# Two layers of spectral mixing and a gated-shift MLP on one core: first norm and transform by group, tables made ahead, sums on two engines, weights over all partitions

## The chip, the cores and the metric

The kernel runs on one core of a Trainium2 chip. TensorE multiplies matrices, VectorE and ScalarE work elementwise and read TensorE's results out of PSUM, GpSimd does small work here, and SyncE (SP) and ScalarE issue the transfers from memory. Each engine works through its own queue in order and waits for others by semaphores. The metric is the device time of one execution in microseconds (us), as a median of several runs.

## The reference, cut to what matters

The state `x` has 2048 rows of 512 numbers in bf16. Two equal layers follow each other. Each layer first mixes by a two-dimensional Fourier transform with a pointwise weight, then runs an MLP block with shifts along the rows:

```
x = x + A(layernorm(x))      # rfft2 over (2048, 512), times (w_r + i w_i), irfft2
x = x + B(layernorm(x))      # h = gelu(layernorm(x) @ w1); quarters of h shifted by -1, +1, -2, +2 rows, @ w2
                             # x1 = x + that; x1 + gelu(layernorm(x1) @ w3) @ w4
x = x + A(layernorm(x))
x = x + B(layernorm(x))
```

## The kernel before

Row p*16 + q of `x` lies in partition p, block q (16 blocks `x[:, q, :]` of 128x512). The transforms are matrix products with tables made on the host: `T` over the partitions, `FA` over the 512 columns, `TL` over the 16 blocks, and their inverses `TR`, `G`, `Tinv`. The norm's mean falls out of the transform, since the zero frequency of the columns is left out; its factor 1/sigma is put into `T`.

`load_all` (line 135) issues all loads: `x` in eight chunks of two blocks on SP's queue (L148), `T` and `FA` on ScalarE's (L149, L150), then on SP's `TL`, the weights `W` in 24 pieces (L157, L159, L161; one destination is 16 neighbouring partitions), `TR`, `G`, `Tinv` and the MLP's matrices. An issue waits until the transfer eight issues earlier has landed.

`first_front` (L253) works in groups of four blocks. For a group it takes the norm's sums, of two blocks in three by `bn_stats` and `bn_aggr` on VectorE (L191, L192), of the third (q % 3 == 2) by two passes of ScalarE over the block (L266) and four small operations of GpSimd (L269 to L272). Then `rstd` (L207): VectorE adds epsilon (`ln_ve`), GpSimd takes the power -1/2 (`ln_r`). One group later, `front` (L234) does for each block a scaled table `Tq` on VectorE (L238), four matmuls into `ps_V` (L241), and a copy into `V`, by turns on VectorE (L244) and ScalarE (L132).

`middle` (L282) has 16 steps b: `over_d` (matmuls from all of `V`, L294), `over_q` (L302 to L304), then in pairs of steps `weigh` (products `Pab` of X with `W` on VectorE, L317, and their sums `Z`), and `back_q` (L326, L327) `LAG = 5` steps later, copied into `M` by turns on ScalarE and VectorE. `X` has two buffers of two steps.

`mlp` (L348) is written out in steps s: `back_d(s)` (`ps_Y`, L366, copied to `Y` by ScalarE), `back_p(s-1)` (`ps_y`, L373; the addition to `x`, L374; `bn`), and after each fourth block `rstd_twice` (L214: VectorE's small operations, two powers on GpSimd giving `ln_r` and `ln_c`). `norm2(g)` scales a group into `xn` (L230) at s = 5, 9, 13, 17, `tr` transposes it (`pt`, copied to `xT` by ScalarE) two steps later, then follow `w1`, `w2`, `norm3`, `apply3`, `tr3`, `w3` and `w4`. With the last four `w4` blocks of the first layer, `fr` calls `front` for the second layer, groups in the order of `GROUPS` (L345): group 0 after the first `w4`, group 1 after the second, groups 2 and 3 after the fourth. Names in the trace are the tiles' names without numbers.

## Time and profile before

| | before |
|---|---|
| median of 3 runs | 437.0 us (434.43 to 437.14) |
| the profiled execution | 437.16 us |
| its span, first to last instruction | 435.4 us |
| TensorE busy (matmul) | 379.7 us, 87% |
| VectorE busy | 215.1 us, 49% |
| ScalarE busy | 214.3 us, 49% |
| GpSimd busy | 39.3 us, 9% |
| mean granted TensorE clock | 0.976 |

The profile is of one execution. Its span leaves out 1.76 us around the instructions. [...] A row's bracket names how long the engine was idle before it and what released it.

### The profile page before, as it was taken

To read this page: it belongs to the slowest core of one execution; us is meant where nothing else is said; L and a number is where in the kernel's file an instruction comes from. 1 tells how busy PE (TensorE), PEld (TensorE's weight loads), DVE (VectorE), ACT (ScalarE), POOL (GpSimd) and SP (SyncE) were. 2 spreads that over 40 slices of the span, in tenths; PEclk is the share of its full clock that TensorE was granted. 3 is DMA by queue.
4 is the path that set the end of the run, shared out by engine and by line. 5 is a ranking of instruction groups with operands and counts; after the bars stand their busy time and mean duration, and the time that the engine had idled before them with its cause. 6 is when DMAs were issued, how large, how long until landed. Compare 5 with 4: busy or idle time off the path is not lost.

```text
span 435.4 us, 5373 instructions
## 1 busy us (share of the span) xinstructions
PE 379.7 (87%) x2048; PEld 189.9 (44%) x2048; DVE 215.1 (49%) x547; ACT 214.3 (49%) x396; POOL 39.3 (9%) x65
## 2 busy tenths in 40 slices
PE   0237997799799999999966998979889999999996
PEld 0123663345345444444433465335444454444442
DVE  4452777987546432231535278698754641011021
ACT  3334774577766814234032576457777680514300
...
DMA packets 12219, 15.63 MB, mean 36 GB/s; under 512 B 1184, under 2 KB 10144, under 8 KB 11936
## 3 DMA queue, kind: packets, MB, share of 16 engines
...
HBM read 13.17 MB, written 2.10 MB: 35 GB/s over the span
## 4 chain that ended last, share of the span: by engine, by line
PE 75%; DVE 9%; DMA 8%; ACT 6%; issue 1%; POOL 0%; ACTq 0%; SPq 0%; DVEq 0%; POOLq 0%
PE ps_g L452 22%; PE ps_o L460 22%; PE ps_TV L294 7%; PE ps_Y L366 5%; PE ps_x L420 4%; PE ps_h L406 4%; DMA W<-in_A_w_r_dram 4%; ACT xT L132 3%; PE pt L393 2%; DVE ln_st L191 2%; DMA TR<-tab_TR 2%; PE ps_X L304 1%; DMA W<-in_A_w_i_dram 1%; DVE x_state L374 1%; PE ps_V L241 1%; ACT junk L425 1%
## 5 line engine op out<-in xcount | busy, mean ns | idle before, releaser
L452 PE MATMUL ps_g<-xT,w 128*128 128x512 bf16 x448 | 100.9, 379 | 3.1 <-ACT xT L132 3.1
L454 ACT ACTIVATE gT<-ps_g 128x512 bf16<-128x512 f32 x112 | 64.7, 604 | 67.9 <-PE ps_g L452 67.9
L460 PE MATMUL ps_o<-w,gT 128*128 128x512 bf16 x448 | 98.0, 379 | 0.0
L462 DVE TENSOR_TENSOR x_state<-ps_o,x_state 128x512 bf16<-128x512 f32 x32 | 22.1, 692 | 125.6 <-PE ps_o L460 125.6
L452 PEld LDWEIGHTS <-w 128*128 128x128 bf16 x448 | 43.6, 98 | 54.9 <-issue 3.7
L460 PEld LDWEIGHTS <-gT 128*128 128x128 bf16 x448 | 43.7, 98 | 52.5
L241 PE MATMUL ps_V<-Tq,x_state 128*128 128x128 bf16 x128 | 13.9, 276 | 34.6 <-DVE Tq L238 34.6
L191 DVE BATCH_NORM_STATS2 ln_st<-x_state 128x6 f32<-128x512 bf16 x59 | 40.8, 691 | 6.1 <-DMA x_state<-in_A_x_dram 4.4
L294 PE MATMUL ps_TV<-FA,V 128*128 128x512 bf16 x128 | 36.8, 418 | 1.6 <-DVE V L244 0.9
L366 PE MATMUL ps_Y<-G,M 128*128 128x512 bf16 x128 | 35.6, 407 | 1.9 <-DVE M L331 0.9
L406 PE MATMUL ps_h<-xT,w 128*128 128x512 bf16 x128 | 33.9, 389 | 2.7 <-ACT xT L132 2.7
L132 ACT ACTIVATE V<-ps_V 128x512 bf16<-128x512 f32 x22 | 12.1, 601 | 48.5 <-PE ps_V L241 48.5
L132 ACT ACTIVATE xT<-pt 128x1024 bf16<-128x1024 bf16 x32 | 31.1, 1032 | 5.3 <-PE pt L393 5.3
L422 DVE SCALAR_TENSOR_TENSOR xn<-xn,ln_c,ps_x 128x512 bf16<-128x512 bf16 x32 | 23.5, 745 | 20.6 <-PE ps_x L420 20.5
L317 DVE TENSOR_TENSOR Pab<-X,W 128x1024 bf16<-128x1024 bf16 x32 | 20.8, 689 | 24.4 <-ACT X L132 24.2
L420 PE MATMUL ps_x<-w,hT 128*128 128x512 bf16 x128 | 32.8, 379 | 0.0
L212 POOL TENSOR_TENSOR ln_r<-ln_ve,mhalf 128x4 f32<-128x4 f32 (+1 forms) x19 | 17.5, 923 | 154.9 <-DVE ln_ve L211 154.9
L425 ACT ACTIVATE junk<-xn 128x512 bf16<-128x512 bf16 x32 | 20.1, 629 | 21.8 <-DVE xn L422 21.7
L132 ACT ACTIVATE TV<-ps_TV 128x512 bf16<-128x512 f32 x32 | 19.1, 597 | 17.9 <-PE ps_TV L294 16.9
L241 PEld LDWEIGHTS <-x_state 128*128 128x128 bf16 x128 | 11.0, 125 | 38.1 <-issue 26.4
L132 ACT ACTIVATE Y<-ps_Y 128x512 bf16<-128x512 f32 x32 | 19.1, 598 | 16.4 <-PE ps_Y L366 16.4
L374 DVE TENSOR_TENSOR x_state<-ps_y,x_state 128x512 bf16<-128x512 f32 x32 | 21.5, 672 | 7.3 <-PE ps_y L373 7.3
...
## 6 DMA issues: line engine op xcount, KB each, us to landing
...
```

What stands on the lines that cost most here:

```text
L132: K.nc.scalar.activation(dst, src, ACT.Copy, bias=0.0, scale=1.0)
L191: v.bn_stats(st[:], src)
L241: nc.tensor.matmul(ps[:, t * P:(t + 1) * P], lhsT=K.x[:, q, t * P:(t + 1) * P], rhs=Tq[:], start=True, stop=True)
L294: nc.tensor.matmul(ps[:], lhsT=V[:, t, b].rearrange("d q c -> d (q c)"), rhs=K.FA[:, t, :], start=(t == 0), stop=(t == 3))
L366: nc.tensor.matmul(ps[:], lhsT=M[:, F, e, q, :], rhs=K.G[:, F, e, :], start=(n == 0), stop=(n == 3))
L374: nc.vector.tensor_tensor(K.x[:, q, :], ps[:], K.x[:, q, :], op=ALU.add)
L406: nc.tensor.matmul(ps[:], lhsT=K.w1[:, t, j * P:(j + 1) * P], rhs=xT[g][:, t, :], start=(t == 0), stop=(t == 3))
L420: nc.tensor.matmul(ps[:], lhsT=K.hT[:, j, st:st + P], rhs=K.w2[:, j, :], start=(j == 0), stop=(j == 3))
L425: nc.scalar.activation(junk[:], xn[:, q, :], ACT.Square, bias=0.0, scale=1.0, accum_out=ln3[g].s[:, i, 1:2])
L452: nc.tensor.matmul(ps[:], lhsT=K.w3[:, c, t * P:(t + 1) * P], rhs=xT3[g][:, c, :], start=(c == 0), stop=(c == 3))
L454: nc.scalar.activation(gT[g][:, t, :], ps[:], ACT.Gelu_apprx_tanh, bias=0.0, scale=1.0)
L460: nc.tensor.matmul(ps[:], lhsT=gT[g][:, t, i * P:(i + 1) * P], rhs=K.w4[:, t, :], start=(t == 0), stop=(t == 13))
```

## The change

Loads: `FA` moves from ScalarE's queue to SP's, behind `x`. The pieces of `W` go to partitions jj*2 + sg, in steps of 8 over all 128, instead of 16 neighbours, and the host's tables `TL` and `TR` follow that order.

First front: all of ScalarE's sums are issued first, for all groups; `scaled_T` (the table), `over_p` (the matmuls) and `take_V` (the copy) take the place of `front`, and the groups interleave, with the four tables of a group made before its matmuls. Copies: two groups by S, S, V, S, two by S, V, S, V.

Norms: `from_sums` and `rstd_twice` run on GpSimd altogether; in `back_p` every odd block's sum comes with the addition (`accum_out`) and its sum of squares from ScalarE. `norm2` comes one step later, and so do the four `apply3`.

`middle`: `LAG` is 6, the last two steps are weighed one by one, and the copies to `M` of the last steps are dealt out anew, the last of them in two halves. Passage to the second layer: tables of groups 0 and 1 before the last four `w4` blocks, of group 2 after the first, and of group 3 one by one; the last copy in two halves.

```diff
-                col = slice(jj * 32 + sg * 16, jj * 32 + sg * 16 + 16)
+                col = slice(jj * 2 + sg, P, 8)
...
     table("T", nc.scalar)
-    table("FA", nc.scalar)
+    table("FA", nc.sync)
     table("TL", nc.sync)
...
-            row = jj * 32
-            nc.sync.dma_start(K.W[row:row + 16, pl, :, :], v[jj])
-            row += 16
-            nc.sync.dma_start(K.W[row:row + 16, pl, 1:16, :], v[7 - jj][:, 1:16, :][:, ::-1, :])
+            rows = slice(jj * 2, P, 8)
+            nc.sync.dma_start(K.W[rows, pl, :, :], v[jj])
+            rows = slice(jj * 2 + 1, P, 8)
+            nc.sync.dma_start(K.W[rows, pl, 1:16, :], v[7 - jj][:, 1:16, :][:, ::-1, :])
...
+    def square(self, i, src):
+        K = self.K
+        junk = K.stream.tile([P, D], BF16, name="junk", bufs=2)
+        K.nc.scalar.activation(junk[:], src, ACT.Square, bias=0.0, scale=1.0, accum_out=self.s[:, i, 1:2])
+
+    def from_sums(self, sl):
+        e = self.K.nc.gpsimd
         t = self.K.small.tile([P, 4, 1], FP32, name="ln_t")
...
+        e.tensor_scalar(self.mv[:, sl], self.s[:, sl], 1.0 / D, None, op0=ALU.mult)
+        e.tensor_tensor(t[:, sl], self.mv[:, sl, 0:1], self.mv[:, sl, 0:1], op=ALU.mult)
+        e.tensor_tensor(self.mv[:, sl, 1:2], self.mv[:, sl, 1:2], t[:, sl], op=ALU.subtract)
...
+        e.tensor_scalar(ve2[:], self.mv[:, :, 1], 0.0, 1.0 + EPS, op0=ALU.max, op1=ALU.mult)
+        e.tensor_scalar(ve2[:], ve2[:], EPS * EPS, None, op0=ALU.add)
+        e.tensor_tensor(self.r[:], ve2[:], K.mhalf[:], op=ALU.pow)
+        e.tensor_scalar(ve[:], self.mv[:, :, 1], 0.0, EPS, op0=ALU.max, op1=ALU.add)
+        e.tensor_tensor(ve[:], ve[:], K.mhalf[:], op=ALU.pow)
+        e.tensor_tensor(ve2[:], ve2[:], self.r[:], op=ALU.mult)
+        e.tensor_tensor(self.c[:], ve2[:], ve[:], op=ALU.mult)
...
+def scaled_T(K, q, r):
+
+    K.Tq[q] = K.stream.tile([P, P], BF16, name="Tq", bufs=NQ)
+    K.nc.vector.tensor_scalar(K.Tq[q][:], K.T[:], r, None, op0=ALU.mult)
...
+def take_V(K, q, eng):
+    src = K.psV.pop(q)[:].rearrange("d (t b c) -> d t b c", t=4, c=8)
+    n = NB // len(eng)
+    for h, e in enumerate(eng):
...
+    for q in on_act:
+        g, i = divmod(q, 4)
+        if not hasattr(L[g], "s"):
+            L[g].sums()
+        junk = K.stream.tile([P, D], BF16, name="junk", bufs=2)
+        nc.scalar.activation(junk[:], K.x[:, q, :], ACT.Copy, bias=0.0, scale=1.0, accum_out=L[g].s[:, i, 0:1])
+        L[g].square(i, K.x[:, q, :])
...
+    def tables(g):
+        for i in range(4):
+            scaled_T(K, 4 * g + i, L[g].r[:, i:i + 1])
+        for i in range(4):
+            over_p(K, 4 * g + i)
+
+    def take(g):
+        for i in range(4):
+            take_V(K, 4 * g + i, "SSVS"[i] if g < 2 else "SVSV"[i])
+
+    stats(0)
+    stats(1)
+    tables(0)
+    stats(2)
+    take(0)
+    tables(1)
+    stats(3)
+    take(1)
+    tables(2)
+    take(2)
+    tables(3)
+    take(3)
...
-        if b % 2 == 1:
-            weigh(b - 1, 2, X)
+        if b >= NB - 2:
+            weigh(b, 1, X[:, b % 2:b % 2 + 1])
+        elif b % 2 == 1:
+            weigh(b - 1, 2, X[:])
...
-    LAG = 5
+    take_M = ["S", "V"] * 5 + ["V", "V", "S", "S", "S", "SV"]
+    LAG = 6
...
+        if i % 2:
+            nc.vector.scalar_tensor_tensor(K.x[:, q, :], ps[:], 1.0, K.x[:, q, :], op0=ALU.mult, op1=ALU.add,
+                                           accum_out=ln[g].s[:, i, 0:1])
+            ln[g].square(i, K.x[:, q, :])
+        else:
+            nc.vector.tensor_tensor(K.x[:, q, :], ps[:], K.x[:, q, :], op=ALU.add)
+            ln[g].bn(i, K.x[:, q, :])
         if i == 3:
+            ln[g].from_sums(slice(1, 4, 2))
             ln[g].rstd_twice()
...
-        g, r = divmod(s - 5, 4)
+        g, r = divmod(s - 6, 4)
         if r == 0 and 0 <= g < 4:
             norm2(g)
...
     if not last:
         new_V(K)
+        for g in range(2):
+            for c in range(4):
+                tables(g, c)
     for i in range(4):
         w4(3, i)
-        if not last and i < 2:
+        if last:
+            continue
+        if i < 2:
             for c in range(4):
                 fr(i, c, "S")
+        if i == 0:
+            for c in range(4):
+                tables(2, c)
+        if i > 0:
+            tables(3, i - 1)
     if not last:
         for c in range(4):
             fr(2, c, "S")
-        for c in range(4):
-            fr(3, c, "SVSV"[c])
+        for c in range(3):
+            fr(3, c, "SSV"[c])
+        tables(3, 3)
+        fr(3, 3, "SV")
```

VectorE's queue in the first front, at the end of the second group's norms, before:

```order
L191 BN_STATS ln_st<-x_state 128x6
L192 BN_AGGR ln_mv<-ln_st 128x2
L211 TENSOR_SCALAR ln_ve<-ln_mv 128x4
L238 TENSOR_SCALAR Tq<-T,ln_r 128x128
L244 CAST V<-ps_V 128x64x8
L238 TENSOR_SCALAR Tq<-T,ln_r 128x128 x2
L244 CAST V<-ps_V 128x64x8
L238 TENSOR_SCALAR Tq<-T,ln_r 128x128
```

The same place now:

```order
L189 BN_STATS ln_st<-x_state 128x6
L190 BN_AGGR ln_mv<-ln_st 128x2
L240 TENSOR_SCALAR Tq<-T,ln_r 128x128 x4
L189 BN_STATS ln_st<-x_state 128x6
L190 BN_AGGR ln_mv<-ln_st 128x2
L189 BN_STATS ln_st<-x_state 128x6
L190 BN_AGGR ln_mv<-ln_st 128x2
L257 CAST V<-ps_V 128x64x8
L240 TENSOR_SCALAR Tq<-T,ln_r 128x128 x4
```

The four tables of a group stand together, `ln_ve` has left VectorE, two norms of the third group stand between the first group's tables and its one copy on VectorE, and the second group's tables follow that copy directly.

VectorE's queue at the passage to the second layer, around the first two of the last four `w4` blocks (L462 is their addition), before:

```order
L462 TENSOR_TENSOR x_state<-ps_o,x_state 128x512
L191 BN_STATS ln_st<-x_state 128x6
L192 BN_AGGR ln_mv<-ln_st 128x2
L211 TENSOR_SCALAR ln_ve<-ln_mv 128x1
L238 TENSOR_SCALAR Tq<-T,ln_r 128x128 x4
L462 TENSOR_TENSOR x_state<-ps_o,x_state 128x512
```

The same place now (L507 is the addition):

```order
L240 TENSOR_SCALAR Tq<-T,ln_r 128x128 x8
L507 TENSOR_TENSOR x_state<-ps_o,x_state 128x512
L189 BN_STATS ln_st<-x_state 128x6
L190 BN_AGGR ln_mv<-ln_st 128x2
L213 TENSOR_SCALAR ln_ve<-ln_mv 128x1
L240 TENSOR_SCALAR Tq<-T,ln_r 128x128 x4
L507 TENSOR_TENSOR x_state<-ps_o,x_state 128x512
```

Eight tables, of groups 0 and 1, stand ahead of the first addition; the four behind it are those of group 2, which were made after the fourth `w4` block.

ScalarE's queue at the start of `mlp`, before:

```order
L132 ACTIVATE Y<-ps_Y 128x512 x8
L132 ACTIVATE xT<-pt 128x4x256 x2
L132 ACTIVATE Y<-ps_Y 128x512
L408 ACT_TABLE_LOAD
L408 ACTIVATE hT<-ps_h 128x4x128
```

The same place now:

```order
L132 ACTIVATE Y<-ps_Y 128x512 x3
L200 ACTIVATE junk,ln_s<-x_state 128x512
L132 ACTIVATE Y<-ps_Y 128x512 x2
L200 ACTIVATE junk,ln_s<-x_state 128x512
L132 ACTIVATE Y<-ps_Y 128x512 x2
L200 ACTIVATE junk,ln_s<-x_state 128x512
L132 ACTIVATE Y<-ps_Y 128x512
L132 ACTIVATE xT<-pt 128x4x256 x2
L132 ACTIVATE Y<-ps_Y 128x512
L200 ACTIVATE junk,ln_s<-x_state 128x512
```

The squares of the odd blocks (L200) stand between the copies of `Y`, each behind the addition on VectorE that it reads.

## Rows read from the trace of the kernel before

**Rows 1.** Windows: stage, us, then busy us (count) of each engine, PEclk, DMA

```profile
0.00:36.80 36.80, 8.66 (x64) 6.38 (x64) 17.45 (x50) 12.28 (x29) 9.67 (x34) 1.00 1.09 236
217.00:239.33 22.33, 14.31 (x106) 8.52 (x106) 11.02 (x34) 7.28 (x14) 2.30 (x4) 0.91 0.00 0
```

**Rows 2.** Sheet of waits, TensorE: us in total, times, longest us

```profile
PE ps_V L241 <- DVE Tq L238: 34.6, 15, 11.7
...
PE ps_g L452 <- ACT xT L132: 3.1, 2, 1.6
```

**Rows 3.** Timeline of the first front: start us, us, engine, operation, [idle before <-releaser]

```profile
25.04 0.62 ACT L266 ACTIVATE junk<-x_state 128x512 bf16<-128x512 bf16 x1
...
26.45 0.23 POOL L269 TENSOR_SCALAR ln_s<-ln_s 128x2 f32<-128x2 f32 x1 [5.09 <-ACT junk L266]
...
26.76 0.19 POOL L270 TENSOR_TENSOR ln_t<-ln_s 128x1 f32<-128x1 f32 x1
...
27.56 0.17 DVE L211 TENSOR_SCALAR ln_ve<-ln_mv 128x4 f32<-128x4 f32 x1 [1.28 <-POOL ln_mv L272]
```

**Rows 4.** Timeline of the passage to the second layer

```profile
219.04 1.05 PE L241 MATMUL ps_V<-Tq,x_state 128*128 128x128 bf16 x16 [2.08 <-DVE Tq L238]
...
232.33 0.69 DVE L462 TENSOR_TENSOR x_state<-ps_o,x_state 128x512 bf16<-128x512 f32 x1 [1.19 <-PE ps_o L460]
...
234.07 1.27 DVE L238 TENSOR_SCALAR Tq<-T,ln_r 128x128 bf16<-128x128 bf16 x6
...
239.33 3.57 PE L294 MATMUL ps_TV<-FA,V 128*128 128x512 bf16 x8 [0.88 <-DVE V L244]
```

**Rows 5.** Timeline, operations whose durations serve as prices

```profile
4.05 0.69 DVE L191 BATCH_NORM_STATS2 ln_st<-x_state 128x6 f32<-128x512 bf16 x1 [4.05 <-DMA x_state<-in_A_x_dram]
...
4.88 0.66 DVE L191 BATCH_NORM_STATS2 ln_st<-x_state 128x6 f32<-128x512 bf16 x1
...
8.92 1.04 POOL L212 TENSOR_TENSOR ln_r<-ln_ve,mhalf 128x4 f32<-128x4 f32 x1 [0.29 <-DVE ln_ve L211]
...
12.34 0.69 DVE L244 CAST V<-ps_V 128x512 bf16<-128x512 f32 x1 [0.68 <-PE ps_V L241]
...
218.75 0.73 DVE L238 TENSOR_SCALAR Tq<-T,ln_r 128x128 bf16<-128x128 bf16 x4
...
219.47 2.06 ACT L132 ACTIVATE V<-ps_V 128x512 bf16<-128x512 f32 x4 [16.97 <-PE ps_V L241]
```

**Rows 6.** Windows while the loads run; the last column is GB/s

```profile
4.00:14.00 10.00, 1.34 (x12) 1.27 (x13) 6.33 (x18) 2.69 (x9) 3.74 (x10) 1.00 1.05 385
14.00:28.00 14.00, 3.02 (x23) 2.10 (x20) 7.22 (x21) 5.92 (x16) 3.73 (x14) 1.00 1.27 118
```

**Rows 7.** Timeline, start of middle: its first matmuls and first product with W

```profile
36.81 3.60 PE L294 MATMUL ps_TV<-FA,V 128*128 128x512 bf16 x8 [0.69 <-ACT V L132]
...
42.98 1.49 DVE L317 TENSOR_TENSOR Pab<-X,W 128x1024 bf16<-128x1024 bf16 x2 [7.52 <-ACT X L132]
```

**Rows 8.** Timeline of SP's queue, one issue of W

```profile
14.54 0.31 SPq L159 DMA_DIRECT2D W<-in_A_w_r_dram  x1
```

**Rows 9.** Sheet of waits, SP's queue: us in total, times, longest us

```profile
SPq L159 <- DMA TL<-tab_TL: 3.8, 1, 3.8
```

**Rows 10.** Windows, TensorE alone: stretch, us, busy us (count), PEclk, DMA, GB/s

```profile
235.40:245.20 9.80, 7.98 (x34) 0.50 0.01 2
```

**Rows 11.** Timeline, start of mlp in the first layer

```profile
69.24 1.89 PE L366 MATMUL ps_Y<-G,M 128*128 128x512 bf16 x8 [0.90 <-ACT M L132]
...
74.46 0.66 DVE L374 TENSOR_TENSOR x_state<-ps_y,x_state 128x512 bf16<-128x512 f32 x1
...
80.17 1.37 PE L393 MATMUL pt<-ident,xn 128*128 128x128 bf16 x16 [2.35 <-DVE xn L230]
```

**Rows 12.** Timeline, a power on GpSimd beside four scalings on VectorE

```profile
103.98 1.17 POOL L227 TENSOR_TENSOR ln_c<-ln_ve,half 128x4 f32<-128x4 f32 x1
...
104.05 1.38 DVE L230 TENSOR_SCALAR xn<-x_state,ln_mv,ln_r 128x512 bf16<-128x512 bf16 x4
```

127 lines of the change are left out of this document (53 added, 74 removed).

## The prediction

> **What bounds the kernel now.** I read the busy time by stage first [rows 1]. TensorE is what the kernel keeps busiest, so only the stages in which it waits have anything to give. Two stand out: the first 36.8 us, in which it is busy 8.66 us, and the passage from the first layer to the second (217 to 239.33), 14.31 of 22.33 us. The sheet of waits names the cause in both: TensorE waited 34.6 us in 15 waits for a scaled table Tq; after that come 3.1 us for a transposed tile xT [rows 2].
>
> The timeline of the first front shows why Tq is late [rows 3]. ScalarE reaches the two sums of block 14 only at 25.04, because it works in order and the copies of the group before stood ahead. GpSimd had waited 5.09 us for those sums, and VectorE's `ln_ve` waits for GpSimd until 27.56, with the next tables queued behind it on VectorE. So the groups run one after the other, some 8 us each, while the data had long landed. At the passage it is another queue: a table whose root was known long before stands on VectorE behind the sum and norm of a `w4` block that has just ended; TensorE idles 2.08 us [rows 4].
>
> **The change part by part. The front.** A chunk of x is 262 KB. The first lands at 4.05 [rows 5], and the rate of those microseconds, 385 GB/s [rows 6], gives 0.68 us for each further one once FA no longer runs beside them: the eighth lands at 8.8. The work then hangs on VectorE's queue. Its prices [rows 5]: a norm some 0.80 us (4.05 to 4.88 for one), four tables 0.73, a copy of V some 0.65 to the next operation (0.69 in the row). Eleven norms (8.8), sixteen tables (2.9) and six copies (3.9) are 15.6 us, from 4.05 to 19.7. In the last two groups VectorE has no norms left to fill the time between its tables and the matmuls of them, and waits some 0.6 and 0.25 us for its two copies: 1.7 us in all, so V is whole at 21.4. The others keep up. ScalarE makes all ten sums first (two passes of 0.62 a block, [rows 3]), done near 11.1, and its ten copies are spaced by 0.52 (four in 2.06, [rows 5]). GpSimd makes the roots out of small operations of about 0.3 us and a power of 1.04 [rows 3, 5]: by 8.6, 10.7, 13.7 and 16.3, where VectorE comes to the tables at 8.9, 11.9, 15.6 and 18.4. The first `ps_TV` moves from 36.81 [rows 7] to 21.4: **15.4 us**. Bounds: 19.7 without any wait (17.1 us), and 23 if x comes one chunk late and each copy waits (13.8 us).
>
> **The weights W.** This decides whether the gain stays. The first product with W ran 6.17 us after the first `ps_TV` (42.98 and 36.81, [rows 7]), so it will want W at 27.6. SP keeps eight transfers in flight; its issue at 14.54 [rows 8], after a wait of 3.8 us for TL's landing [rows 9], shows when W gets the engines. FA on SP's queue changes nothing here: the same bytes stand ahead. W is 2.1 MB, and from 14 to 28 us the load ran at 118 GB/s, against 385 before it [rows 6]. At 118 W is whole at 14.5 + 17.8 = 32.3; at 385, at 20.0. In time means at least 2.1 MB in 13.1 us, 160 GB/s. The stretch at 385 writes all 128 partitions in each transfer, the one at 118 sixteen neighbours; the change spreads each over all of them and keeps its 512-byte pieces. I take it to be in time, cost nothing, and keep 118 as the far end: W 4.7 us late, of which some 0.7 is slack in the two X tiles, so 4 us, with TR behind it. [...]
>
> **The passage.** The tables of groups 0 to 2 are now made while `w4` still runs, so the wait of 2.08 us at 219.04 [rows 4], and two more like it, go. From 217.0 TensorE does `ps_V` of four blocks (0.9 us), `w4` (3.0), four blocks (0.9), two `w4` (6.1), four blocks (0.9), two blocks (0.45): 229.3. The end hangs on the last `w4` block, done at 228.0: sum and norm as now, 1.74 us until the next table (232.33 to 234.07, [rows 4]), 0.3 to its matmul (218.75 to 219.04), 0.43 to the copy (219.04 to 219.47, [rows 4, 5]), a copy of 0.65, the last table 0.3, matmul 0.45, half a copy 0.4: 232.4. Now the second layer's `ps_TV` starts at 239.33 [rows 4]: **6.9 us**. Bounds: 6.2 (the three waits alone) and 7.5.
>
> **The clock.** [...] The end of the new passage is still thin (2.5 us idle of its last 3.2), so I expect a fall there too, at the usual price of some 2 us: **0.9 us** gained, between 0 and 2.9.
>
> **Sums split with ScalarE.** `back_p` of odd blocks sums in the addition, so two norms of 0.80 [rows 5] in each group leave VectorE, and ScalarE gets a square of 0.63 + 0.1 instead. What waits is the first transpose, 10.93 us after the first `ps_Y` (80.17 and 69.24), on VectorE's `xn` [rows 11]. Its addition takes 0.66 [rows 11]: VectorE is done with four blocks after 6.9 instead of 8.3 us, but the root now comes after the square (0.7) and GpSimd's five small operations and a power (2.5): at 10.2, and the transpose at 10.7. Nothing is gained there, and what was a wait for VectorE becomes one for GpSimd. Eight squares a layer are 5.8 us more on ScalarE, in a stage where TensorE already waits for its xT [rows 2]; behind it in the queue are Y and xT copies. I put **0.5 us** a layer on it, 1.0 in all (0 to 2). `norm3` on GpSimd adds some 0.2 us to a root that is used one step later now: nothing. The tail of `middle` (lag 6, last pairs weighed singly) shifts about as much work as it saves: nothing, within 1 us a layer.
>
> **GpSimd beside VectorE.** More small operations run on GpSimd while VectorE scales tiles. A power of GpSimd at 103.98 took 1.17 us instead of 1.04, and the four scalings beside it, from 104.05, 1.38 [rows 12]: both went on, at a price of 0.15. In the sum that is nothing. [...]
>
> **The sum.** 15.4 + 6.9 + 0.9 - 1.0 = 22.2 us. The profiled execution took 437.16 (span 435.4 and 1.76 around it; the median of the runs is 437.0, so nothing is to be corrected). 437.16 - 22.2 = 415.0.
>
> **The rivals.**
> (a) W keeps its pace: if the 512-byte pieces and not the partitions made the 118 GB/s [rows 6]. Against it: nothing but the destination's shape is known to differ so much; for it: no row has such pieces at another rate. Price 4 us: 419.
> (b) GpSimd's chain holds up the scalings. Behind the root it still has a small operation, a power and two small ones to do for `ln_c`, 1.9 us; if VectorE's scalings of the first group wait for them, in each layer, 3.8 us: 418.8. The rows of the scalings beside a power speak against it [rows 12]. [...]
> (c) The front is not pipelined: the tables still wait for the roots, since sums, norms and small operations on three queues couple again, as in [rows 3]. With two groups at the present 8 us, V is whole near 30: 423.6.
> (d) Slower than before: the spread rows load more slowly than the neighbours did. The gain is gone when W comes 22 us after 27.6, that is when 2.1 MB take 35 us, below 60 GB/s; at 50 GB/s W lands at 56.5 and the time is near 443. The 385 GB/s on all 128 partitions [rows 6] speak against it.
>
> **How the numbers follow.** The forecast has 0.70, (a) 0.14, (b) 0.07, (c) 0.06, (d) 0.03. Its own range, with the bounds of the front, of the passage, the clock and ScalarE, is 410 to 418. (a) and (b) lie at 419 give or take 1.5; with them the range is 409 to 421, and (c), (d) and a tenth of the forecast stay outside, some 2 in 10. About 1% (4.4 us) is what a measurement of this kernel can tell from no change. All cases but (d) are faster by more: 0.95; within 1% needs a rate of W between 55 and 65 GB/s or several mishaps, 0.02; slower 0.03.
>
> **What would show it.** Right: first `ps_TV` near 21 us, TensorE's waits for Tq down from 34.6 to under 12 us with the first of them ending near 9; first product with W within 6.5 us of it; no wait for Tq after the first three `w4` of the last group, and the second layer's first `ps_TV` some 15 us after 217 on the old scale; xn waited for by GpSimd's root, not VectorE's norms. Wrong: VectorE's first product waiting for a transfer of W (then a), scalings that begin only as GpSimd's `ln_c` ends (b), VectorE idle for GpSimd between groups of the front (c). The forecast falls as a whole if W's load still shows near 118 GB/s, or if ScalarE is what TensorE waits for through the stretch after the transform by more than 2 us a layer.

## The result, and the profile after

The changed kernel takes 407.9 us (median of four runs, 407.18 to 413.24) against 437.1 for the kernel before: a ratio of 0.937 (95% interval 0.928 to 0.946), 29.2 us less, where the prediction had 22.2. Run again its median was 412.2 (ratio 0.942, 0.937 to 0.946), because its executions fall into two groups, five of ten at 407.2 to 408.7 and five at 411.6 to 414.7; over all ten the median is 410.2. The experiments say what the upper group most likely is. The profiled execution took 407.92 us, span 406.1, and is of the lower group; what follows is worked out from it.

The windows of the two stages that the prediction spoke of, the first front and the passage, in the kernel after. Columns: stage, us, then busy us (count) of each engine, granted clock (TensorE's, as a share of its full speed), DMA share, GB/s:

```profile
0.00:21.20 21.20, 7.46 (x64) 6.65 (x64) 15.06 (x44) 13.03 (x31) 9.70 (x32) 1.00 0.86 255
201.40:216.60 15.20, 12.99 (x107) 7.62 (x104) 8.89 (x26) 7.56 (x15) 2.54 (x5) 1.00 0.00 0
```

Against [rows 1] the front is 21.2 us instead of 36.8, with 2.4 us less work on VectorE and 0.75 more on ScalarE, and the passage 15.2 instead of 22.33. TensorE's and VectorE's waits, in the sheet of waits (us in total, times, longest):

```profile
PE ps_V L247 <- DVE Tq L240: 12.9, 5, 9.1
...
DVE Pab L351 <- DMA W<-in_A_w_i_dram: 8.5, 2, 6.2
...
PE ps_h L452 <- ACT xT L132: 3.9, 6, 1.1
...
PE ps_M L360 <- DMA TR<-tab_TR: 1.9, 1, 1.9
```

The wait for Tq was 34.6 us in [rows 2] and is 12.9, of which 9.1 are the start, up to the first group's tables. One more wait of 1.86 us, ahead of the third group's `ps_V`, is put down to a transfer of W that those matmuls don't read; with it the wait is 14.7. A wait is there that the kernel before did not have, TensorE's 1.9 us for TR. The timeline of the front and the start of `middle`:

```profile
8.82 0.73 DVE L240 TENSOR_SCALAR Tq<-T,ln_r 128x128 bf16<-128x128 bf16 x4
...
15.90 0.55 SPq L159 DMA_DIRECT2D W<-in_A_w_r_dram  x1
...
21.27 3.57 PE L326 MATMUL ps_TV<-FA,V 128*128 128x512 bf16 x8 [0.83 <-ACT V L132]
...
26.83 0.58 SPq L142 DMA_DIRECT2D TR<-tab_TR  x1
...
27.34 0.69 DVE L351 TENSOR_TENSOR Pab<-X,W 128x1024 bf16<-128x1024 bf16 x1 [6.17 <-DMA W<-in_A_w_i_dram]
30.36 0.69 DVE L351 TENSOR_TENSOR Pab<-X,W 128x1024 bf16<-128x1024 bf16 x1 [2.33 <-DMA W<-in_A_w_i_dram]
...
33.67 0.27 PE L360 MATMUL ps_M<-TR,Z 128*128 128x256 bf16 x1 [1.86 <-DMA TR<-tab_TR]
```

The first `ps_TV` is at 21.27 (36.81 in [rows 7]). The product with W's first plane runs at 27.34, as X comes (ScalarE's copy of it ends at 27.31; the transfer that the row names is not what it waited for). For the second plane VectorE then waits 2.33 us, until 30.36, and TensorE waits for TR, which SP issues at 26.83, until 33.67. Once TL has landed, SP's issues of W take 0.55 to 0.61 us each, where the kernel before had 0.31 to 0.42 [rows 8].

The start of the first layer's `mlp` and the second layer's first `ps_TV`:

```profile
64.26 0.63 ACT L200 ACTIVATE junk<-x_state 128x512 bf16<-128x512 bf16 x1 [0.79 <-DVE x_state L417]
...
65.02 1.38 DVE L233 TENSOR_SCALAR xn<-x_state,ln_mv,ln_r 128x512 bf16<-128x512 bf16 x4 [0.85 <-POOL ln_r L226]
65.07 0.40 POOL L227 TENSOR_SCALAR ln_ve<-ln_mv 128x4 f32<-128x4 f32 x1
65.49 1.36 PE L439 MATMUL pt<-ident,xn 128*128 128x128 bf16 x16 [1.18 <-POOL ln_ve L227]
...
216.61 1.90 PE L326 MATMUL ps_TV<-FA,V 128*128 128x512 bf16 x8 [0.48 <-ACT V L132]
```

The first transpose comes 10.69 us after the first `ps_Y` (54.80); VectorE's scalings start as GpSimd's root ends and run beside GpSimd's next operations. At 216.61 eight `ps_TV` take 1.90 us, at a granted clock of 1.00; in [rows 4] they took 3.57, where [rows 10] shows 0.50. The mean granted clock of this execution is 1.00. One thing that figure leaves out: the first eight `ps_TV`, at 21.27, take 3.57 us, the half pace, and so did those of the kernel before (3.60, [rows 7]), although the windows of both fronts show 1.00. The trace has no record of the clock ahead of 24.8 us here (40.5 before), so for the first front the spacing of the matmuls is what counts.

Read stage by stage, from the first instruction of a kind in the timelines (us; "middle" is first `ps_TV` to first `ps_Y`, "mlp start" first `ps_Y` to first `w3`), the gain stands where the prediction put it only in part. `w3` is `ps_g` in the trace. The other lines are the experiments below:

| kernel | first ps_TV | middle 1 | mlp start 1 | second ps_TV | middle 2 | mlp start 2 |
|---|---|---|---|---|---|---|
| before | 36.81 | 32.43 | 50.35 | 239.33 | 33.87 | 51.69 |
| after | 21.27 | 33.53 | 49.25 | 216.61 | 29.84 | 49.24 |
| passage put back | 21.82 | 33.56 | 49.26 | 226.78 | 29.83 | 49.23 |
| sums put back | 21.37 | 36.12 | 52.11 | 222.16 | 29.85 | 52.13 |
| sums and norm2 put back | 21.93 | 36.34 | 48.86 | 219.69 | 29.84 | 48.85 |
| norm2 put back | 21.43 | 32.95 | 53.80 | 220.74 | 29.85 | 55.45 |
| W put back | 21.33 | 36.93 | 49.24 | 220.06 | 31.52 | 49.23 |
| front put back | 35.43 | 32.61 | 49.20 | 229.80 | 29.84 | 49.23 |
| before, TensorE kept busy at the passage | 37.15 | 32.53 | 50.34 | 238.76 | 30.92 | 52.09 |
| TR on ScalarE's queue | 21.45 | 38.78 | 49.54 | 222.33 | 29.84 | 49.23 |
| the same, TensorE kept busy in the front | 20.11 | 41.29 | 49.53 | 223.49 | 31.52 | 49.23 |
| loads in another order | 22.33 | 31.89 | 49.23 | 216.01 | 29.84 | 49.22 |
| the same, TensorE kept busy in the front | 20.79 | 30.55 | 49.24 | 213.13 | 29.85 | 49.22 |

From before to after: front 15.5, middle 1 -1.1, mlp start 1 1.1, passage 7.1 (from the end of the first of the last four `w4` blocks to the second `ps_TV`, 22.3 to 15.2), middle 2 4.0, mlp start 2 2.45; the rest is alike. That is 29.1 us.

### The profile page after: what moved, and what is told of

The parts are those of the page before. It is cut to its first block, busy times and chain, and to the rows that moved or that the text cites. A ratio compares the mean times of both kernels' runs of the same rounds, so it can differ in the third digit from the quotient of the medians.

```text
span 406.1 us, 5436 instructions
## 1 busy us (share of the span) xinstructions
PE 370.3 (91%) x2048; PEld 187.2 (46%) x2048; DVE 189.1 (47%) x458; ACT 225.2 (55%) x433; POOL 63.6 (16%) x162
## 4 chain that ended last, share of the span: by engine, by line
PE 74%; DVE 7%; ACT 6%; DMA 4%; SPq 3%; issue 2%; POOL 1%; ACTq 0%; DVEq 0%
PE ps_g L497 24%; PE ps_o L505 24%; PE ps_x L466 5%; PE ps_TV L326 5%; PE ps_h L452 5%; PE ps_Y L405 4%; ACT xT L132 4%; DMA TL<-tab_TL 3%; PE pt L439 2%; DMA TR<-tab_TR 2%; DVE Pab L351 1%; DVE xn L468 1%; PE ps_y L412 1%; PE ps_X L336 1%; PE ps_M L360 1%
## 5 line engine op out<-in xcount | busy, mean ns | idle before, releaser
L507 DVE TENSOR_TENSOR x_state<-ps_o,x_state 128x512 bf16<-128x512 f32 x32 | 22.1, 691 | 120.9 <-PE ps_o L505 120.9
L497 PEld LDWEIGHTS <-w 128*128 128x128 bf16 x448 | 43.6, 98 | 54.9 <-issue 3.7
L452 PE MATMUL ps_h<-xT,w 128*128 128x512 bf16 x128 | 32.8, 379 | 3.9 <-ACT xT L132 3.9
L326 PE MATMUL ps_TV<-FA,V 128*128 128x512 bf16 x128 | 34.2, 394 | 1.3 <-ACT V L132 1.3
L405 PE MATMUL ps_Y<-G,M 128*128 128x512 bf16 x128 | 32.5, 379 | 1.5 <-DVE M L369 0.8
L189 DVE BATCH_NORM_STATS2 ln_st<-x_state 128x6 f32<-128x512 bf16 x43 | 29.6, 688 | 5.1 <-DMA x_state<-in_A_x_dram 4.0
L200 ACT ACTIVATE junk<-xn 128x512 bf16<-128x512 bf16 x32 | 20.2, 630 | 20.5 <-DVE xn L468 20.5
L205 POOL TENSOR_SCALAR ln_mv<-ln_s 128x4 f32<-128x4 f32 (+2 forms) x21 | 5.7, 272 | 162.6 <-ACT junk L200 162.4
L351 DVE TENSOR_TENSOR Pab<-X,W 128x1024 bf16<-128x1024 bf16 (+1 forms) x36 | 21.2, 627 | 20.2 <-ACT X L132 11.7
L132 ACT ACTIVATE V<-ps_V 128x512 bf16<-128x512 f32 (+1 forms) x25 | 12.9, 592 | 25.7 <-PE ps_V L247 25.7
L247 PE MATMUL ps_V<-Tq,x_state 128*128 128x128 bf16 x128 | 11.8, 263 | 14.7 <-DVE Tq L240 12.9
L452 PEld LDWEIGHTS <-w 128*128 128x128 bf16 x128 | 12.2, 98 | 18.6 <-issue 5.6
L405 PEld LDWEIGHTS <-M 128*128 128x128 bf16 x128 | 12.3, 98 | 18.1 <-issue 2.4
## 6 DMA issues: line engine op xcount, KB each, us to landing
w<-in_B_w_dram SPq DMA_DIRECT2D x2, 1792.0 KB, 14.7
```

The source lines that it names most:

```text
L132: K.nc.scalar.activation(dst, src, ACT.Copy, bias=0.0, scale=1.0)
L189: v.bn_stats(st[:], src)
L326: nc.tensor.matmul(ps[:], lhsT=V[:, t, b].rearrange("d q c -> d (q c)"), rhs=K.FA[:, t, :], start=(t == 0), stop=(t == 3))
L351: nc.vector.tensor_tensor(t[pl][:, 0:n], X, K.W[:, pl, sl].unsqueeze(2).to_broadcast([P, n, 2, 256]), op=ALU.mult)
L405: nc.tensor.matmul(ps[:], lhsT=M[:, F, e, q, :], rhs=K.G[:, F, e, :], start=(n == 0), stop=(n == 3))
L452: nc.tensor.matmul(ps[:], lhsT=K.w1[:, t, j * P:(j + 1) * P], rhs=xT[g][:, t, :], start=(t == 0), stop=(t == 3))
```

## The experiments

### One part put back: the passage

```diff
     def fr(g, i, eng):
+        tables(g, i)
         over_p(K, GROUPS[g][i])
         take_V(K, GROUPS[g][i], eng)
...
-        for g in range(2):
-            for c in range(4):
-                tables(g, c)
```

(and the calls of `fr` behind the `w4` blocks as in the kernel before.)

> The changed kernel (407.9 us), with only the passage to the second layer put back: each table is made directly ahead of its matmuls, so VectorE's sum and norm of the last w4 block stand ahead of it again. Theory 1 (the waits for Tq at the passage cost 7.1 us, and the idle time of TensorE there is what brought the granted clock to 0.50 in the kernel before): the second layer's first ps_TV comes 7 us later in the same frame, a stretch at 0.50 shows again from a few us ahead of it, eight ps_TV take 3.57 us instead of 1.90, and the time is 407.9 + 7.1 + 2.9 = 418. Rival (the clock's falls do not follow from this idle time, but differ from one execution to another or come from the start of the MLP block): the waits return, the clock stays at 1.00, 415.

Measured: 417.7 us (416.95 to 419.77), ratio 0.958 (0.953 to 0.963). The waits returned, and a fall of the clock with them, but at another place than expected. Timeline of TensorE, and windows (stretch, us, busy us (count), granted clock, DMA, GB/s), in this kernel:

```profile
204.09 1.05 PE L247 MATMUL ps_V<-Tq,x_state 128*128 128x128 bf16 x16 [2.08 <-DVE Tq L240]
204.98 4.87 PE L505 MATMUL ps_o<-w,gT 128*128 128x512 bf16 x14
211.93 1.73 PE L247 MATMUL ps_V<-Tq,x_state 128*128 128x128 bf16 x16 [2.08 <-DVE Tq L240]
213.45 7.24 PE L505 MATMUL ps_o<-w,gT 128*128 128x512 bf16 x28
```

```profile
206.00:208.00 2.00, 2.00 (x6) 0.50 0.00 0
```

The first wait of 2.08 us is followed by 0.50 here, and so is the second, with 0.53 from 212 to 214; in the kernel before two such waits passed at 1.00 and the fall came behind the third [rows 4, 10]. A `w4` block takes 4.87 instead of 3.19, the next `ps_V` 1.73 instead of 1.05, two `w4` 7.24 instead of 6.21: the falls cost 3.4 us, and the second `ps_TV` is late by 10.2, of which 0.6 come from the layer before. So the waits themselves are 6.2, at the lower bound of the prediction's term. The size of the first theory stands (418); that the clock falls near the end of the passage does not.

### One part put back: the split of the sums

```diff
-        if i % 2:
-            nc.vector.scalar_tensor_tensor(K.x[:, q, :], ps[:], 1.0, K.x[:, q, :], op0=ALU.mult, op1=ALU.add,
-                                           accum_out=ln[g].s[:, i, 0:1])
-            ln[g].square(i, K.x[:, q, :])
-        else:
-            nc.vector.tensor_tensor(K.x[:, q, :], ps[:], K.x[:, q, :], op=ALU.add)
-            ln[g].bn(i, K.x[:, q, :])
+        nc.vector.tensor_tensor(K.x[:, q, :], ps[:], K.x[:, q, :], op=ALU.add)
+        ln[g].bn(i, K.x[:, q, :])
         if i == 3:
-            ln[g].from_sums(slice(1, 4, 2))
```

> The changed kernel with only the split of the sums in back_p put back: all sixteen norms of that stage are made by bn_stats on VectorE, the squares leave ScalarE; the small operations stay on GpSimd and norm2 keeps its place. Theory 1 (the prediction's step: eight squares a layer cost 0.5 us of waiting behind ScalarE's queue, and nothing is gained at the first transpose): 406.9, clock 1.00 throughout. Rival (the split is what keeps TensorE from idling in one piece ahead of the first transpose, and so keeps the clock at 1.00): VectorE's norms come late again, TensorE idles over 2 us at one place in the first 12 us after the first ps_Y, the clock falls to 0.50 for some 3.5 us behind it in each layer, price 1.7 us a layer: 410 to 411.

Measured: 414.5 us (413.18 to 416.35), ratio 0.950 (0.946 to 0.955). The rival held, and more. Timeline and windows of this kernel:

```profile
68.79 1.35 DVE L233 TENSOR_SCALAR xn<-x_state,ln_mv,ln_r 128x512 bf16<-128x512 bf16 x4
...
69.23 1.78 PE L432 MATMUL pt<-ident,xn 128*128 128x128 bf16 x16 [3.15 <-POOL ln_ve L229]
```

```profile
65.50:69.20 3.70, 0.57 (x3) 1.00 0.00 0
69.20:73.00 3.80, 3.77 (x22) 0.55 0.00 0
```

The root was ready at 67.6 (GpSimd's power ran from 66.58), but with `norm2` one step later the addition and the norm of one more block stand ahead of the scalings on VectorE, until 68.79. TensorE idles 3.15 us in one piece and works at half clock behind it: mlp start 52.1 in both layers instead of 49.25, of which the fall is 1.7 (0.45 of 3.77 us busy). The execution shown also lost 2.6 us in middle 1, behind a wait for TR and a fall of the clock, though nothing ahead of `mlp` was changed:

```profile
34.68 0.27 PE L360 MATMUL ps_M<-TR,Z 128*128 128x256 bf16 x1 [2.65 <-DMA TR<-tab_TR]
```

So this alone does not say what the split is worth. The next two runs complete the square.

### Split and `norm2` put back together, and `norm2` alone

```diff
-        g, r = divmod(s - 6, 4)
+        g, r = divmod(s - 5, 4)
```

once on top of the kernel above, once on the changed kernel.

> The changed kernel with the split of the sums put back (all norms of that stage on VectorE) and norm2 one step earlier again, as in the kernel before; the small operations stay on GpSimd. Theory 1 (the split is worth something by itself: it takes TensorE's idle time ahead of the first transpose apart, and the clock stays at 1.00; norm2's later place only suits it): the first transpose 10.4 to 10.9 us after the first ps_Y, 2.3 us idle ahead of it in one piece, a stretch at 0.50 behind it in each layer, 1.7 us each: 411.5, between the changed kernel and the one with the split alone put back (414.5). Rival (the place of norm2 has no part in it): 414.5 again. Second rival (the split is worth nothing, and the 6.6 us came from norm2's later place alone): 407 to 408.

> The changed kernel with the split of the sums kept and only norm2 one step earlier, as in the kernel before. Theory 1 (the root comes 10.2 us after the first ps_Y either way, and VectorE's scalings wait for it): VectorE stands still some 2 us longer ahead of them, the additions of the two next blocks come behind them, the transpose comes at the same 10.7, and what is lost is under 1 us a layer: 408 to 409.5. Rival (with the additions late TensorE has nothing left to do and idles in one piece, and the clock falls as in the kernel before): 411 to 412.

Measured with both put back: 410.3 us (409.84 to 411.96), ratio 0.941 (0.936 to 0.946). Its timeline:

```profile
68.89 1.36 PE L432 MATMUL pt<-ident,xn 128*128 128x128 bf16 x16 [2.04 <-POOL ln_ve L227]
```

The transpose is 10.62 us after the first `ps_Y`, the idle 2.04 us, and the clock stays at 1.00 behind it in both layers. The mlp start takes 48.86 and 48.85, 0.4 us a layer **less** than in the changed kernel. What makes the total larger is middle 1 with 36.34, a wait of 2.5 us for TR and a fall behind it (`ps_M` takes 0.42 us from 37.66 on, 0.27 at 35.45), and a front 0.7 longer; the edit touches neither. None of the three theories is right as it stood; the total agreed with the first for a wrong reason.

Measured with `norm2` alone early: 418.6 us (418.07 to 420.22), ratio 0.960 (0.956 to 0.964), far beyond both expectations. Timeline and sheet of waits of this kernel:

```profile
64.59 1.38 DVE L233 TENSOR_SCALAR xn<-x_state,ln_mv,ln_r 128x512 bf16<-128x512 bf16 x4 [1.43 <-POOL ln_r L226]
...
66.67 0.63 ACT L200 ACTIVATE junk<-x_state 128x512 bf16<-128x512 bf16 x1 [3.62 <-DVE x_state L417]
...
67.78 1.93 ACT L132 ACTIVATE xT<-pt 128x1024 bf16<-128x1024 bf16 x2
...
69.75 1.02 PE L452 MATMUL ps_h<-xT,w 128*128 128x512 bf16 x4 [1.45 <-ACT xT L132]
```

```profile
PE ps_h L452 <- ACT xT L132: 10.1, 8, 1.6
```

VectorE waits at the scalings for GpSimd's root; the addition of an odd block stands behind them; ScalarE waits 3.62 us at that block's square; and the copies of Y and xT stand behind the square. Three engines wait for each other in a ring, and TensorE waits 10.1 us for xT instead of 3.9: mlp start 53.8 and 55.45. So the later `norm2` is not an extra of the change: with the split it is worth 4.6 and 6.2 us (1.7 of the 6.2 is a fall of the clock, from 266.05 on, with 0.75 from 267 to 272), without it it costs 3.3 a layer (1.7 of that the fall shown above). The two edits belong together, and together they are worth nothing here, or -0.4 us a layer.

### One part put back: W in neighbouring partitions

```diff
-            rows = slice(jj * 2, P, 8)
+            rows = slice(jj * 32, jj * 32 + 16)
...
-            rows = slice(jj * 2 + 1, P, 8)
+            rows = slice(jj * 32 + 16, jj * 32 + 32)
```

(and the order of the columns in TL and TR with it.)

> The changed kernel with only the destinations of W (and the order in TL and TR that follows it) put back to sixteen neighbouring partitions. Theory 1 (the rate of the transfers decides: 118 GB/s for neighbours): after TL has landed at 15.9 the seventeen pieces left take 0.73 us each as before, the last lands near 33.5, TR is issued near 29 and lands near 36.5; the first product of plane i waits until 33.5, TensorE waits for TR some 4.8 us instead of 1.9: 410.8. Rival (SP's own time for an issue decides: 0.60 us for the spread pieces, 0.31 to 0.41 for neighbours): the pieces go out faster, TR is issued by 22 to 24 and lands by 31, TensorE does not wait for it: 406.

Measured: 409.9 us (407.68 to 413.0), ratio 0.940 (0.933 to 0.947): not told apart from the changed kernel by time. Its executions are of two groups too (407.68 and 408.25; 411.64 and 413.0), and the profile is one of the upper: 

```profile
35.44 0.27 PE L360 MATMUL ps_M<-TR,Z 128*128 128x256 bf16 x1 [3.25 <-DMA TR<-tab_TR]
```

```profile
31.00:35.40 4.40, 1.19 (x7) 1.00 0.98 392
35.40:39.20 3.80, 3.76 (x15) 0.55 1.08 363
```

TensorE waits 3.25 us for TR and is at half clock behind it, middle 1 is 3.4 us longer than after; middle 2 with 31.52 had a fall too (1.7). What the partitions do to the transfer shows in the windows of W's load, SP's line of each (last columns DMA share and GB/s), first after, then W put back:

```profile
16.50:26.80 10.30, 1.00 0.61 135
```

```profile
16.40:26.80 10.40, 1.00 1.15 138
```

The rate is the same, 135 and 138 GB/s, but the spread pieces keep the transfer engines busy for 0.61 of the time instead of 1.15. By the DMA issues of each, a piece of plane i of 128 KB lands in 3.0 us instead of 5.2:

```profile
W<-in_A_w_i_dram SPq DMA_DIRECT2D x4, 128.0 KB, 3.0
```

```profile
W<-in_A_w_i_dram SPq DMA_DIRECT2D x4, 128.0 KB, 5.2
```

So a piece did land in some 0.6 of the time, with the transfer engines busy about half as long; why, the runs don't show. But the limit moved to SP, which needs 0.60 us for each spread piece and 0.31 to 0.42 for one into sixteen neighbours (the kernel before, from 14.54 on). In the changed kernel its issues of W from 15.90 on follow each other with 0.64 us between them in all sixteen steps together, so SP is what sets their pace; with W put back it is 3.3 us, most of them waits for the landing of earlier transfers. TR is issued at 26.83 and 26.85. Both theories were half right. W's last piece lands at 30.2 with the spread rows and at 31.8 without; how much of the longer wait for TR comes from that, these two executions don't say, since the wait differs as much between executions that load alike (0.6 us in the second profile of the changed kernel, 2.65 with the sums put back).

### One part put back: the first front

The old `first_front`: a group's sums behind the copies of the group before, tables, matmuls and copies block by block.

```diff
-    tables(0)
-    stats(2)
-    take(0)
-    tables(1)
...
+        if prev:
+            for i in range(4):
+                scaled_T(K, 4 * g - 4 + i, prev.r[:, i:i + 1])
+                over_p(K, 4 * g - 4 + i)
+                take_V(K, 4 * g - 4 + i, "VS"[i % 2])
```

> The changed kernel with only the order of the first front put back: ScalarE's sums of a group stand behind the copies of the group before, tables, matmuls and copies go block by block, one group behind the norms. Theory 1 (the order on ScalarE and VectorE is the whole of the 15.5 us): the first ps_TV comes at 36 to 37 instead of 21.3, TensorE waits for Tq over 30 us again, W and TR have long landed so that the 1.9 us for TR go: 407.9 + 15.5 - 1.9 = 421.5. Rival (a part of the gain comes from x's transfers no longer sharing the engines with FA, and from one operation less on VectorE a group): the first ps_TV near 34 and 418.5.

Measured: 420.7 us (420.27 to 421.27), ratio 0.964 (0.959 to 0.969). The first `ps_TV` is at 35.43:

```profile
35.43 3.60 PE L311 MATMUL ps_TV<-FA,V 128*128 128x512 bf16 x8 [0.69 <-ACT V L132]
```

That is 14.2 us later than after and 1.4 earlier than before. The order of the queues, with VectorE's `ln_ve` of each group, is 14.2 of the 15.5 us, and with W and TR long there the four executions lie within 1.0 us. The other 1.4 are the rival's: `FA` no longer lands beside the start of `x` (it lands at 5.9 us in the kernel before, at 11.2 in the kernel after). ScalarE's first sum, before and in this kernel:

```profile
6.12 0.63 ACT L266 ACTIVATE junk<-x_state 128x512 bf16<-128x512 bf16 x1 [3.24 <-DMA x_state<-in_A_x_dram]
```

```profile
4.72 0.63 ACT L281 ACTIVATE junk<-x_state 128x512 bf16<-128x512 bf16 x1 [2.30 <-DMA x_state<-in_A_x_dram]
```

The second chunk of `x` lands at 4.70 instead of 6.10, and the whole chain behind it, VectorE's first `ln_ve` (7.28, 8.66) and the first `ps_TV` too, comes 1.4 us sooner.

### The clock by itself: the kernel before with TensorE kept busy at the passage

```diff
+def warm(K, n):
+    ps = bank(K, "ps_d")
+    for _ in range(n):
+        K.nc.tensor.matmul(ps[:], lhsT=K.ident[:], rhs=K.FA[:, 0, :], start=True, stop=True)
...
         if not last and i < 2:
+            warm(K, 9)
             for c in range(4):
                 fr(i, c, "S")
```

(nine more ahead of group 2, four and three at the end; their result is not read.)

> The kernel before with nothing changed but matmuls without use (identity by FA, 512 columns, result not read) put into TensorE's waits at the passage: nine ahead of each of the three groups of ps_V that wait 2.08 us, four ahead of the next one, three ahead of ps_TV. VectorE's and ScalarE's work and the waits for it stay. Theory (the idle time at the passage brings the granted clock down to 0.50 from 235.4 to 245.2, and the clock has a price of its own): no 0.50 there, the eight ps_TV take 1.9 us instead of 3.57, the stage to the next ps_Y about 30.5 instead of 33.9: 437.1 - 3.4 = 433.7. Rival (the fall has another cause, or the chip falls later in its place, in the next thin stretch): 437.

Measured: 433.8 us against 437.1, ratio 0.995 (0.992 to 0.998). The medians differ by 3.3 us; by the ratio it is 2.3, because some executions of the kernel before lie at 433.9 to 435.7, with a granted clock of 0.984 to 0.986, and the rest at 437 to 438, with 0.976 to 0.980. Timeline and windows of this kernel:

```profile
234.81 1.51 PE L241 MATMUL ps_V<-Tq,x_state 128*128 128x128 bf16 x24
...
238.76 1.89 PE L300 MATMUL ps_TV<-FA,V 128*128 128x512 bf16 x8 [0.44 <-DVE V L244]
```

```profile
235.40:245.20 9.80, 9.27 (x65) 1.00 0.01 2
```

The tables come when they came before, but the stretch that stood at 0.50 in [rows 10] is at 1.00, and middle 2 takes 30.92 us instead of 33.87: the fall behind the passage costs 2.95 us in `middle` by itself. The passage, counted from the first `w3` of the first layer, is 1.0 us shorter too (118.74 instead of 119.74; 112.56 after): that is the part of the fall that lies ahead of the second `ps_TV`. The run also gives the tail of `middle` its price: at full clock 30.92 with the old tail, 29.84 with the new one.

### TR ahead: two ways

On ScalarE's queue:

```diff
-    for k in ("TR", "G", "Tinv"):
+    K.table = table
+    for k in ("G", "Tinv"):
...
     take(1)
+    K.table("TR", nc.scalar)
     tables(2)
```

> The changed kernel once more, as the base for the three beside it on the same chip: 407.9 us, ratio 0.937. Some executions may lie near 413, where TensorE's wait for TR of 1.9 us is longer and the granted clock falls to 0.50 behind it (theory from the run with W put back, where a wait of 3.25 us had that behind it); if those executions have nothing to do with TR, they show up as often in the kernel with TR ahead.

> The changed kernel with the load of TR issued on ScalarE's queue behind the copies of the second group (near 14.7 us, where ScalarE waits 1.7 us for TensorE) instead of on SP's behind all of W (26.83). Theory (SP's 0.65 us for each of the 24 pieces of W is what makes TR late, not the rate of the transfers, which have room beside W): TR lands by 26, TensorE's wait of 1.9 us for it goes, W is whole at 30 to 31 as before, the wait for Z that takes its place is under 0.5 us: 406.2, and no execution near 413. Rival (the transfers' rate is the limit, so 1.6 MB more beside W push it back by up to 4 us): the product of plane i waits until 33 to 34, TensorE waits 2 to 4 us for Z: 408 to 410.

Measured: the changed kernel 412.2 (407.67 to 414.71, both groups), this one 415.3 (412.6 to 416.12), ratio 0.952 (0.948 to 0.955): slower, on the rival's side, but by more than it had and by another mechanism. The sheet of waits of SP's queue and VectorE's timeline:

```profile
SPq L161 <- DMA TR<-tab_TR: 6.5, 1, 6.5
```

```profile
36.46 0.69 DVE L353 TENSOR_TENSOR Pab<-X,W 128x1024 bf16<-128x1024 bf16 x1 [7.35 <-DMA W<-in_A_w_i_dram]
```

TR itself is there at 23.5. But from another queue it takes one of the eight places in flight all the same: SP stands still for its landing, VectorE has W's second plane at 36.46 instead of 30.36, and TensorE waits 4.78 us for Z, with a fall of the clock at its end (0.50 from 37.6 to 40.3). The matmuls without use in the first front on top of it:

> The kernel with TR on ScalarE's queue, and matmuls without use in TensorE's waits of the first front: two ahead of the second group's ps_V, four ahead of the third's, two ahead of the fourth's, two ahead of the first ps_TV. Theory (the first ps_TV run at half pace, eight in 3.57 us against 1.90 in the second layer, because TensorE had been little busy in the front): they take some 1.9 us now and ps_V of the last groups 1.05 instead of 1.86: about 1.7 us less than the kernel with TR alone, 404.5, as far as W (whole at 30.3) and TR then come in time; if they don't, what is gained comes back as a wait for Z, and the time stays near 406. Rival (the pace at the start has nothing to do with what TensorE did before): eight ps_TV in 3.57, 406.2 or a little more.

Measured: 416.3 us (412.84 upward; one execution, at 666, stands apart), ratio 0.952. The first half held: `ps_TV` at 20.11, eight in 1.89 us. The second half, the gain, was lost in the wait for W, whose second plane VectorE had only at 36.67, and in a fall of the clock that begins during that wait (the first `ps_M` behind it already take 0.40 us each, 0.27 in the changed kernel; the releaser that TensorE's row names, G, is another transfer that landed then):

```profile
20.11 1.89 PE L337 MATMUL ps_TV<-FA,V 128*128 128x512 bf16 x8 [0.59 <-DVE V L258]
...
37.88 0.40 PE L371 MATMUL ps_M<-TR,Z 128*128 128x256 bf16 x1 [8.97 <-DMA G<-tab_G]
```

Then the loads in another order, all on SP's queue, so that no transfer of 1.6 MB stands among the eight:

```diff
-    table("TL", nc.sync)
...
+    def part(k, b0, b1):
+        nc.sync.dma_start(getattr(K, k)[:, b0:b1, :], dram[k][:, b0:b1, :])
...
     for pl, w in enumerate((A_w_r, A_w_i)):
...
+        part("TL", 4 * pl, 4 * pl + 4)
+    part("TR", 0, 4)
+    part("TL", 8, 12)
+    part("TR", 4, 8)
+    part("TL", 12, 16)
+    part("TR", 8, 16)
```

> The changed kernel with the loads in another order, all on SP's queue: FA, the twelve pieces of W's first plane, a quarter of TL, the second plane, a second quarter of TL, then quarters of TR and TL by turns. So no transfer of 1.6 MB stands among the eight that may be in flight (SP stood still from 12.0 to 15.9 us for TL, and in the run with TR on ScalarE's queue from 17.0 to 23.5 for TR). Theory (TR is late by 1.9 us because SP's issues, 0.65 us each, and that standstill push it back, and in the executions near 412 the granted clock falls behind this wait): W's last piece is issued near 21.5 and all of W there by 25, TensorE's wait for TR goes, nothing over 0.5 us takes its place: 406.0, all executions within 1 us. Rival (the executions near 412 have another cause): 406 in some and 410 to 412 in others.

Measured: 406.7 us (406.4 to 406.9 in six executions), ratio 0.932 (0.929 to 0.935). The timeline:

```profile
25.68 0.43 SPq L156 DMA_DIRECT2D TR<-tab_TR  x1
...
28.78 1.29 DVE L362 TENSOR_TENSOR Pab<-X,W 128x1024 bf16<-128x1024 bf16 x2 [6.54 <-ACT X L132]
```

VectorE's first products wait for X alone, TensorE's wait for TR is gone, and so is the upper group. W's last issue is only at 24.41, not 21.5, and the front is 1.1 us slower than after (first `ps_TV` 22.33), which takes back part of the gain: the third chunk of `x` lands at 7.41 instead of 5.93 and VectorE waits 0.94 us for it. W's pieces are now issued where TL was, beside the end of `x`; that they are the reason is not shown: the next run issues its loads in the same order and has its third chunk at 5.96.

> The kernel with the loads in the other order, and matmuls without use in TensorE's waits of the first front (two, four, two and two, as in the run that had TR on ScalarE's queue, where the first ps_TV came at 20.11 instead of 21.27, eight of them took 1.89 instead of 3.57, and the last ps_X ahead of the wait ended 2.9 us earlier). Theory (there the gain was lost to W, whole only at 36; here W and TR are in time): 406.0 - 2.9 = 403.1. Rival (W at 25 is now too late for the earlier products, or TL's first quarter for the earlier ps_X at 21.9): 404 to 406.

Measured: 405.1 us (403.83 to 406.06), ratio 0.928 (0.925 to 0.932): the fastest kernel here, some 2 us short of the theory. The timeline names where:

```profile
12.09 1.01 PE L276 MATMUL ps_d<-FA,ident 128*128 128x512 bf16 x2 [0.96 <-DMA FA<-tab_FA]
...
20.79 1.89 PE L346 MATMUL ps_TV<-FA,V 128*128 128x512 bf16 x8 [0.59 <-DVE V L268]
...
28.46 0.28 PE L354 MATMUL ps_X<-TV,TL 128*128 128x256 bf16 x1 [0.60 <-DMA TL<-tab_TL]
```

The matmuls without use wait for FA and so push `ps_V` back, and TL's second quarter is 0.6 us late: the loads again. This is the fastest of the six executions, 403.83; three of the others have a granted clock of 0.996 instead of 1.00, so part of what the median lacks is most likely a fall of the clock, in executions that were not profiled.

## Why the prediction was right, and where it was not

**The front: right.** 15.5 us against 15.4. One step of the sum was wrong without harm: the eighth chunk of `x` was to land at 8.8 once FA no longer ran beside it, and lands at 9.97, as before (10.01); the second chunk is what came sooner, and VectorE waited only for the first. The four groups of tables started at 8.82, 11.65, 15.28 and 18.18 where 8.9, 11.9, 15.6 and 18.4 were worked out from the prices of [rows 5]. The front put back cost 14.2 us of it; rival (c) is out. The sign "waits for Tq under 12 us" was missed, with 12.9, or 14.7 with the wait that the sheet puts down to W; the time of the first `ps_TV` shows that this did not matter.

**The passage: right, with a mixed term.** 7.1 against 6.9 (the prediction's steps add up to 232.3, not 232.4, so 7.0). Put back, its waits were 6.2, and the kernel before with TensorE kept busy there has 6.2 to gain too: the lower bound, the three waits alone. The other 1.0 is the half clock ahead of the second `ps_TV`, for which the prediction had no term. So the nearness of 7.1 to 6.9 is in part luck.

**The clock: the step that failed, in size.** The prediction had one fall in view, the one behind the passage ([rows 10]; at 0.50, half of the 5.9 us from 239.33 to 245.2 is 2.9, the term's upper bound), expected it to stay in a cheaper form, at a "usual price of some 2 us", and put the difference, 0.9 us, on it. No run shows that price: the fall went altogether in the execution shown, and where one came behind the changed passage, in two other kernels, it cost 1.7 us (middle 2 31.52 instead of 29.84). Three more went that the sum had no term for. Windows of the kernel before, TensorE alone:

```profile
81.00:85.00 4.00, 4.00 (x17) 0.57 0.00 0
272.00:276.00 4.00, 3.05 (x10) 0.58 0.00 0
286.00:290.00 4.00, 4.00 (x20) 0.57 0.00 0
```

Busy time by the missing share of the clock gives 1.7, 1.3 and 1.7 us, 4.7 in all, and the fall behind the passage 2.95 (measured with TensorE kept busy there). 7.65 instead of 0.9 is 6.75 us more, nearly all of the 7.0 by which the gain was larger than predicted. These rows could have been read beforehand: the granted clock of the whole span, not that of one stretch. They are of one execution; others of the kernel before, at 433.9 to 435.7 us, have a higher clock and so less to gain.

That such falls go when TensorE's work closes up is shown for the passage by the matmuls without use (1.00 from 235.4 to 245.2 with them, 0.50 without). For the start of `mlp` it is shown one way only: 2.35 us of idle ahead of the transpose in the kernel before and 3.15 us with the sums put back had a fall behind them, in both layers, and 2.04 us (two layers) and the changed kernel's pieces of 0.53 and 1.18 us had none. With split and `norm2` both put back the falls stay away too, so it was not those two edits that took them away; what that run keeps of the change there is GpSimd's part, the small operations of the norm, and this was not tried by itself. What removed the fall at 272, behind waits of 1.35 and 0.95 us, no run shows: about the same waits in the first layer had none behind them.

No rule can be read off the length of a wait. One of 2.08 us at the passage had a fall behind it in the run with the passage put back, and in the kernel before two had none behind them and the third one; and in two executions the passage as changed had a fall behind it after all (middle 2 31.52). What else decides where the clock falls, the runs here don't show.

**The sums and ScalarE: right, in the sum and in place.** 0.5 us a layer was put on the squares; split and later `norm2` together cost 0.4, and TensorE's waits for xT, 3.9 us in two layers, stay just within the 2 us a layer that the prediction set as a sign. The transpose was to come at 10.7 us, held by GpSimd's root: 10.69. What the prediction missed is how much hangs on the two edits being made together: either alone costs 5.7 or 10.8 us in the two mlp starts, the falls of the clock behind its waits included.

**W: the step was wrong, at a small price.** "In time, cost nothing" needed 160 GB/s; W moved at 135, the second plane came 2.8 us after the 27.6 at which the prediction wanted it, and TR behind it made TensorE wait 1.86 us. The prediction weighed rate against rate, the 118 read against the 160 needed, and left out what each issue costs on SP's queue. SP's 0.6 us for each of 24 pieces became the limit. Nor was 118 a fixed price of sixteen neighbours: with W put back they moved at 138. Rival (a) gave the right kind of wait, 4 us by its sum, of which 1.9 came. In the upper group of executions it is most likely this wait with a fall behind it. The wait differs between executions that load alike: in the profiles of kernels with the changed kernel's loads and first layer up to `mlp` it was 0.2 to 1.9 us in four, with no fall behind it, and 2.5 and 2.65 in two, with one, and from the first `ps_M` to `ps_Y` the six took 21.1 and 22.8 us. Every execution of the upper group has a granted clock of 0.988 to 0.996, every one of the lower group 0.999 or 1.00, and with the loads in the other order the group is gone. No execution of the changed kernel's own upper group was profiled, so this is not shown directly; why TR lands at 33.2 in one execution and at 35.4 in another is open.

**The tail of `middle`:** put at nothing within 1 us a layer; it is worth 1.1 in the second (30.92 to 29.84 at full clock). In the first, `middle` is 1.1 longer with a wait of 1.9 for TR in it, so about 0.8 shows there. TensorE's last two waits are 0.83 and 0.74 us in the first layer instead of 1.35 and 0.90.

**GpSimd beside VectorE: right.** Scalings of 1.38 us from 65.02, GpSimd's small operation at 65.07 took 0.40 instead of some 0.25, and its power at 65.56, also beside them, 1.07: both engines went on, as in [rows 12], and rival (b) is out. Rival (d) is out by W's 135 GB/s.

So with the terms as measured: 15.5 + 7.1 + 7.65 (clock) + 2.2 (tail) - 1.9 (TR) - 0.8 (squares) = 29.75, against 29.1 in the stage table; where the last 0.6 are is open. The result lies below the range because the clock's bounds, 0 to 2.9, were drawn round one fall of four.
